# Memory rows in two groups, half copies, weights by chunk: one change to a fused attention and gated-FFN kernel

## The chip, the cores and the metric

The kernel runs on one core of one Trainium2 chip. The time is device microseconds of one execution; before the change three executions took 1120.69, 1125.61 and 1126.81 us, median 1125.61. A separate execution was profiled. Engines are named as in the profile: PE is the matrix engine (PEld its weight loads), DVE the vector engine, ACT the scalar engine, POOL the GpSimd engine, SP the sync engine, which issues most transfers. A "q" after an engine's name means the transfers that it issues.

## The reference

`x` is (2048, 640). A layer norm is followed by attention with a recurrent memory, a residual sum, a second layer norm, a gated FFN and a second residual sum:

```python
mem = mem0                                        # 8 rows
for s in range(64):                               # segments of 32 tokens
    h = concat([mem, xs])                         # 40 rows, 640 wide
    q, k, v = h @ Wq, h @ Wk, h @ Wv              # 32 heads of 128
    p = softmax(where(mask, q @ k.T * scale, -1e9))
    o = (p @ v) @ Wo
    mem = o[:, :8]                                # goes into the next segment
    outs.append(o[:, 8:])
h2 = h + (relu(xn @ W_gate) * (xn @ W_up)) @ W_down    # xn = layernorm(h), F = 1728
```

All weights and results are bf16. Only the 8 memory rows are serial: segment s+1 can't begin before the 8 rows of segment s have been through the output projection.

## The kernel before, in words

Everything is written by hand as a list of operations with keys of what they read and write. `_Graph.solve` turns the keys into semaphore waits, and each engine runs its operations in the order in which they were added. There is no scheduler: an operation that waits holds everything behind it on its engine. PSUM keys are whole banks (512 fp32 columns), and one bank's readers on different engines follow each other in program order.

**Start.** SP loads the first 64 and the next 128 rows of x, then the projection weights W (K, Q, V, each in two halves of 2560 KB) and the output weights Wo (two halves of 2560 KB), in this order on one queue. ACT issues the load of mem0. The first segments' tokens are normalised and projected while the weights come in.

**Passes.** One pass per segment, `s` = 0 to 63, in the loop over `NSEG`. A pass holds the 8 memory rows plus 24 token rows ("riders") of later segments, so that 32 columns of the array are filled; the tokens' last quarter is done by `extra_units` as filler. In PE's order a pass is: project K (`project`, 5 chunks of 128 rows x 2 halves x 4 matmuls of 512 columns), project Q, project V chunks 0 and 1, `pick_mem` (the memory rows' Q), V chunks 2 to 4, `scores`, two filler parts, `pv_mem` (first part with Vr, the older tokens' V; second with Vp, the memory rows' own), two filler parts, `trans_om` (transposes of the attention result of the memory rows into PSUM), a last filler part, `wo_pass` (the output projection, 128 small matmuls in two halves of 64), `pv_x` (attention of the segment's tokens). The next pass begins with K. In passes with `s % 4 == 1` the filler is `woe_pass`; in the others it is one of the three projections of the last quarter of tokens.

**What the other engines do in between.** After `scores`, ACT takes the exponentials of the memory part (`exp_mem`, into om), copies V bank P2 into Vp (`to_v`), and takes the exponentials of the token part (`exp_x`); DVE masks the first into Pbd in two instructions, one for each part of `pv_mem`. DVE copied V bank P3 into Vp before that. After `trans_om` DVE copies the transposes into oT in one instruction; `wo_pass` waits for it. After `wo_pass` `to_act` transposes the 160 columns of its result on DVE (`TBf`) and casts the 8 memory columns of each of the 5 chunks into `act_r`; the next pass's K waits for that. ACT stores the row form (`wtok`), DVE normalises `pv_x`'s result (`norm_x`: rx, then ox twice) and then copies half of K's result (`tok`) when K is done. K, Q and ox are turned around by transposing transfers on SP's queue (KS, QS, oT). POOL issues the copies of the riders' V rows (`v_riders`).

**PE's instruction stream.** `align` pads PE's stream with spare weight loads so that multiples of 256 instructions fall at chosen places (`MARKS`). In the DMA part of the profile the instruction queue carries 202 packets and 3.31 MB, which is one packet of 16 KB per 256 instructions of PE.

**Tail.** In pass 62 POOL loads the FFN's gate and up weights over the Q weights (`load_gate_up`: xn2T, Wg, Wgu, Wu, Wgu). After pass 63's attention PE runs the output projection of pass 62 (source QS, in two halves with a transpose between), that of pass 63 (source oT), the last `woe_pass`, and then four `gate_up` groups of block 0. SP loads the rows of block 1, and POOL h and the down weights, when Wu has landed.

**FFN.** Four blocks of 512 tokens. `gate_up` makes 14 chunks of 128 hidden units; the last holds 64 and takes partitions 64 to 127. `down` sums the 14 chunks for 128 tokens in two halves of 320 columns. In chunks 0 to 12 the second half is issued by `again`, which uses the weights already loaded; chunk 13 works on 64 partitions and loads its weights for each half.

Of the kernel before, what the change touches and what calls it, by code (L numbers as in the profile page):

```python
# [206 lines left out]
def build_kernel(nc, A_x, A_mem0, A_Wq, A_Wk, A_Wv, A_Wo, A_seg_len, B_W_gate, B_W_up, B_W_down, out):  # L207
# [134 lines left out]
    add("dve", lambda v: v.memset(oT[:], 0.0), w=[("oT", "m"), ("oT", "x")])  # L342
    add("pool", lambda p: p.memset(ap(Vp, Dh, [[VW, 8], [1, VW - Dh]]), 1.0), w=[("Vp1",)])
    for i in range(2):
        add("pool", lambda p, i=i: p.memset(act_r[i][:], 0.0),
            w=[("act", i, j, "m") for j in range(4)] + [("act", i, "x")])
# [82 lines left out]
    def to_v(b, t, i, key, eng):  # L429
        copy_op(eng, v_dst(t, i), bank(b).rearrange("p (k d) -> p k d", d=128), [B(b)], [key])  # L430

    def v_dst(t, i):
        return ap(t, 4 * i * VW, [[VW, 4], [1, 128]])
# [53 lines left out]
    def v_riders(t0, n):  # L487

        done = 0
        while done < n:  # L490
# [3 lines left out]
            for g in range(4):  # L494
                a, z = 32 * g + M + done, 32 * (g ^ 1) + o
                dma(Vr[q][z:z + m, :, :], Vp[a:a + m, :, :], r=[("Vp",), ("Vp1",), ("Vr1", q)],
                    w=[("Vr", q, g, o)], eng="pool")
# [8 lines left out]
    def ln1_load(b, buf, key):  # L506
        t0, n = (0, 64) if b < 0 else (64 + 128 * b, min(128, S - 64 - 128 * b))
        dma(buf[0:n, :], x_ap[t0:t0 + n, :], w=[key])
# [4 lines left out]
    def ln1_back(b, src, r, eng):  # L513
# [8 lines left out]
        if b < 0:  # L522
            for e in range(2):
                copy(act_r[1][:, e, :, :], src[:, :, 32 * e:32 * e + 32], [("act", 1, e, "m"), ("act", 1, "x")])
            return
# [11 lines left out]
    def pass_act(s):  # L537
        b, j = s // 4, s % 4
        return act_r[b % 2][:, j], [("act", b % 2, j, "m"), ("act", b % 2, "x", j), ("act", b % 2, "x")]
# [5 lines left out]
    def to_act(s, wkey, src):  # L545

        b, j = s // 4, s % 4
        add("dve", lambda v: v.transpose(TBf[:].rearrange("p c t -> p (c t)"), src), r=[wkey], w=[("TBf",)])  # L548
        add("dve", lambda v: v.tensor_copy(act_r[b % 2][:, j, :, 0:M], TBf[:, :, 0:M]), r=[("TBf",)],  # L549
            w=[("act", b % 2, j, "m")])  # L550
# [42 lines left out]
    def pv_mem(s):  # L593
        q = seg_slot(s)
        for a in range(2):
# [8 lines left out]
            add("pe", f, r=[("Pbd", a)] + ([("Vp",), ("Vp1",)] if a else vr_keys(q)), w=[B(T1)])  # L604
# [7 lines left out]
    def trans_om(tile):  # L612
        def f(pe):
            for a in range(2):
                for c in range(0, 128, tile):
                    i = pe.matmul(bank_bf(T1)[c:c + tile, a * 128:(a + 1) * 128], om[:, a, c:c + tile],  # L616
                                  ident[:, :], is_transpose=True)
            return i
        add("pe", f, r=[("om",), ("ident",)], w=[B(T1)])
        copy_op("dve", ap(oT, 0, [[2 * SEG, 8], [16 * SEG, 2], [SEG, 2], [1, M]]),  # L620
                bank_bf(T1)[:, 0:256].rearrange("p (k g e q) -> p k g e q", k=8, g=2, e=2), [B(T1)], [("oT", "m")])
# [8 lines left out]
    def wo_pass(bk, mark=None, src=oT, keys=(("oT", "m"), ("oT", "x")), halves=(0, 1)):  # L630
        for hf in halves:
# [7 lines left out]
            op = add("pe", f, r=list(keys) + [("Wo", hf)], w=[B(bk)])  # L639
# [24 lines left out]
    def pv_x(s, b0):  # L664
# [16 lines left out]
        add("pe", f, r=[("Px",), ("Pbd", 0), ("Pbd", 1), ("Vp",), ("Vp1",)] + vr_keys(q), w=[B(b0 + g) for g in range(4)])  # L681
# [11 lines left out]
    def trans_ox():  # L693
        dma_t(oT[:].rearrange("p h t -> p (h t)").rearrange("p (k r) -> p k r", r=128),
              ox[:].rearrange("p k g d -> p (k g d)"), [("ox", 0), ("ox", 1)], [("oT", "m"), ("oT", "x")])
# [14 lines left out]
    def copy_oTe(s):  # L710
        o = M * (s % 4)
        copy_op("dve", oTe[:, :, o:o + M], oT[:, :, 0:M], [("oT", "m")], [("oTe", s % 4)])
# [13 lines left out]
    def ln2_load(i):  # L726
        u = i % 4
        dma(xt2[u][:, :], x_ap[128 * i:128 * i + 128, :], r=[("Wdone", 1), ("Wu",)], w=[("xt2", u)])
        load_attn(at2[u], i, [("Wdone", 1), ("Wu",)], ("at2", u))
# [14 lines left out]
    ln1_load(-1, xt, ("xt",))  # L744
    ln1_load(0, x0, ("oTe", 0))
# [32 lines left out]
    a0, k0 = pass_act(0)  # L778
    groups = [(a0, k0)] + [(act_r[1][:, e], [("act", 1, e, "m"), ("act", 1, "x")]) for e in range(2)]
# [38 lines left out]
    for i in range(2):  # L818
        for n, (a, ks) in enumerate(groups):
            q = seg_slot(n - 1)  # L820
            t, key = (Vr[q], ("Vr", q)) if n else (Vp, ("Vp",))
# [364 lines left out]
```

## Time and profile before

| | us |
|---|---|
| median of three executions | 1125.61 |
| profiled execution, its own time | 1116.98 |
| its span | 1115.3 |
| start, up to 64 us: PE busy | 33.80 of 64.00 |
| passes 1 to 61 and the beginning of 62, 64 to 904 us: PE busy | 829.46 of 840.00 |
| change-over, 904 to 931 us: PE busy | 20.36 of 27.00 |
| FFN, 931 to 1116 us: PE busy | 180.32 of 185.00 |

PE's busy time overlaps itself, since matmuls are pipelined: a row "0.39 PE ... x4" is four matmuls of 512 columns in four column groups at once, and the next four start 0.22 us later. So waits of PE are read from the distance between starts and not from the busy share. In the timeline a row has its start, its length, engine, line, operation, what it writes and reads, the tile, and, in brackets, the idle time of that engine before it with what ended it. Line 397 is the reuse of loaded weights in `again`, and lines 461 (DVE) and 459 (ACT) are the copies in `copy_op`, so these are told apart by their tiles.

### The profile page before, as it was taken

To read this page: it belongs to the slowest core of one execution; us is meant where nothing else is said; L and a number is where in the kernel's file an instruction comes from. 1 tells how busy PE (TensorE), PEld (TensorE's weight loads), DVE (VectorE), ACT (ScalarE), POOL (GpSimd) and SP (SyncE) were. 2 spreads that over 40 slices of the span, in tenths; PEclk is the share of its full clock that TensorE was granted. 3 is DMA by queue.
4 is the path that set the end of the run, shared out by engine and by line. 5 is a ranking of instruction groups with operands and counts; after the bars stand their busy time and mean duration, and the time that the engine had idled before them with its cause. 6 is when DMAs were issued, how large, how long until landed. Compare 5 with 4: busy or idle time off the path is not lost.

```text
span 1115.3 us, 55631 instructions
## 1 busy us (share of the span) xinstructions
PE 1063.9 (95%) x28054; PEld 508.5 (46%) x23495; DVE 594.2 (53%) x1479; ACT 354.7 (32%) x732; POOL 286.3 (26%) x575
## 2 busy tenths in 40 slices
PE   4679999999999999999999999999999988999998
PEld 3344444444544454445454444444444455343443
DVE  3235555565556565666565656565656552463422
ACT  2213333334333333333333333333343422131220
POOL 1013333333333332323232323241424231000000
PEclk9979999999999999999999999999999999999999
DMA  9935464645454645465555565555545465122100
GB/s 352 380 85 106 91 109 85 105 90 107 85 108 82 109 80 111 80 124 102 117 106 112 107 111 111 98 102 96 100 92 92 88 198 178 42 77 77 24 18 24
DMA packets 287656, 121.61 MB, mean 109 GB/s; under 512 B 263840, under 2 KB 277056, under 8 KB 287424
## 3 DMA queue, kind: packets, MB, share of 16 engines
q1 hardware_dynamic: 268048, 94.16, 39.2%
q0 software_dynamic: 19184, 23.89, 9.4%
q8 instruction: 202, 3.31, 1.2%
q14 instruction: 30, 0.25, 0.1%
q10 hardware_dynamic: 192, 0.01, 0.0%
HBM read 36.79 MB, written 7.21 MB: 39 GB/s over the span
## 4 chain that ended last, share of the span: by engine, by line
PE 86%; DMA 6%; DVE 4%; SPq 3%; issue 1%; ACT 0%; DVEq 0%; ACTq 0%
PE ps L419 24%; PE ps L397 23%; PE ps L636 13%; PE ps L1021 10%; PE ps L1054 3%; PE ps L564 3%; PE ps L650 3%; SPq L357 3%; DMA QS<-tok 3%; DMA Wo<-in_A_Wo_dram 3%; PE ps L601 2%; DVE TBf L548 2%; PE ps L448 2%; PE ps L616 1%; DVE act_r L549 1%
## 5 line engine op out<-in xcount | busy, mean ns | idle before, releaser
L419 PE MATMUL ps<-W,act_r 128*32 128x512 bf16 x4277 | 395.0, 383 | 14.8 <-DMA W<-in_A_Wq_dram 3.0
L397 PE MATMUL ps<-W,act_r 128*32 128x512 bf16 x3603 | 352.6, 379 | 0.0
L357 POOL DMA_DIRECT2D Vr<-Vp x376 | 187.5, 506 | 466.9 <-ACT Vp L459 292.8
L419 PEld LDWEIGHTS ps<-W,act_r 128*32 128x32 bf16 x4277 | 115.4, 97 | 272.5 <-issue 213.3
L459 ACT ACTIVATE tok<-ps 128x512 bf16<-128x512 f32 x191 | 110.3, 594 | 257.0 <-PE ps L397 223.2
L461 DVE CAST tok<-ps 128x512 bf16<-128x512 f32 x131 | 90.6, 691 | 146.7 <-PE ps L397 121.5
L636 PE MATMUL ps<-Wo,oT 128*32 128x160 bf16 x8192 | 158.8, 236 | 10.3 <-DMA Wo<-in_A_Wo_dram 7.9
L636 PEld LDWEIGHTS ps<-Wo,oT 128*32 128x32 bf16 x8192 | 144.4, 98 | 36.0 <-DVE oT L461 24.9
L419 PE MATMUL ps<-W,act_e 128*32 128x512 bf16 x900 | 90.9, 381 | 0.0
L397 PE MATMUL ps<-W,act_e 128*32 128x512 bf16 x900 | 90.5, 379 | 0.0
L689 DVE TENSOR_TENSOR ox<-ps,rx 128x512 bf16<-128x512 f32 x128 | 82.5, 686 | 2.2
L459 ACT ACTIVATE Qr<-QS 128x512 bf16<-128x512 bf16 (+3 forms) x107 | 70.0, 682 | 31.7 <-DMA QS<-tok 31.2
L357 POOL DMA_DIRECT2D attn_d<-wtok x64 | 46.6, 729 | 115.0 <-ACT wtok L459 115.0
L548 DVE STREAM_TRANSPOSE TBf<-ps 128x160 f32<-128x160 f32 x64 | 22.4, 350 | 95.2 <-PE ps L636 95.1
L1021 PE MATMUL ps<-xn2T,Wg 128*128 128x512 bf16 x260 | 64.6, 379 | 0.0
L1021 PE MATMUL ps<-xn2T,Wu 128*128 128x512 bf16 x260 | 64.6, 379 | 0.0
L1036 DVE TENSOR_TENSOR hT<-g,ps 128x512 bf16<-128x512 bf16 (+1 forms) x56 | 38.5, 687 | 48.5 <-PE ps L1021 44.6
L574 ACT ACTIVATE om<-ps 128x128 bf16<-128x128 f32 x63 | 17.5, 277 | 146.0 <-PE ps L564 143.4
L1054 PE MATMUL ps<-Wd,hT 128*128 128x320 bf16 (+1 forms) x240 | 63.3, 300 | 0.0
L1034 ACT ACTIVATE g<-ps 128x512 bf16<-128x512 f32 (+1 forms) x56 | 32.4, 592 | 94.2 <-PE ps L1021 94.1
L461 DVE CAST Vp<-ps 128x512 bf16<-128x512 f32 x64 | 44.3, 692 | 31.0 <-PE ps L397 25.5
L397 PE MATMUL ps<-Wd,hT 128*128 128x320 bf16 x208 | 56.9, 299 | 0.0
(112 smaller groups left out, 1161.6 us busy)
## 6 DMA issues: line engine op xcount, KB each, us to landing
Vr<-Vp POOLq DMA_DIRECT2D x124, 48.8 KB, 1.9
W<-in_A_Wk_dram SPq DMA_DIRECT2D x2, 2560.0 KB, 13.4
W<-in_A_Wq_dram SPq DMA_DIRECT2D x2, 2560.0 KB, 25.6
W<-in_A_Wv_dram SPq DMA_DIRECT2D x2, 2560.0 KB, 27.3
Wo<-in_A_Wo_dram SPq DMA_DIRECT2D x2, 2560.0 KB
xt<-in_A_x_dram SPq DMA_DIRECT2D x30, 160.0 KB, 3.6
Vr<-Vp POOLq DMA_DIRECT2D x128, 32.5 KB, 1.9
attn_d<-wtok POOLq DMA_DIRECT2D x64, 40.0 KB, 2.8
```

Of the source, the lines that this page charges most:

```text
L357: add(eng, lambda e: e.dma_start(dst, src), r=r, w=w, dma=True)
L397: return pe.add_instruction(mybir.InstMatmult(name=nc.get_next_instruction_name(), engine=mybir.EngineType.PE, ins=[pe.lower_ap(rhs), pe.l ...
L419: ins = pe.matmul(*a, start=(c == 0), stop=(c == DC - 1), skip_group_check=True)
L459: add("act", lambda a: a.activation(dst, src, ACTF.Copy), r=r, w=w)
L461: add("dve", lambda v: v.tensor_copy(dst, src), r=r, w=w)
L548: add("dve", lambda v: v.transpose(TBf[:].rearrange("p c t -> p (c t)"), src), r=[wkey], w=[("TBf",)])
L564: i = pe.matmul(bank((P0, P1)[g % 2])[p:p + (M if a else 32), 40 * k:40 * k + 40], lh, Qr[:, h, q, :], start=True, stop=True, skip_group_c ...
L636: i = pe.matmul(bank(bk)[32 * gg:32 * gg + 32, 0:160], src[:, hb, :], w[:, gg], start=(hb == ORDER[0]), stop=(hb == ORDER[31]), skip_group ...
L689: add("dve", lambda v, kh=kh: v.tensor_tensor(ox[:, :, kh, :], src[:, :, kh, 0:128], ap(rx, kh, [[2, 4], [0, 128]]), ALU.mult), r=[B(b0 + ...
L1021: ins = pe.matmul(bank(bk), w[:, c, lo:lo + 128], xn2T[par][:, c, :], start=(c == 0), stop=(c == DC - 1))
L1036: add("dve", lambda v: v.tensor_tensor(hT[par][lo:128, j, :], g1[gi][lo:128, :], bank(bu)[lo:128, :], ALU.mult), r=[B(bu), ("g1", gi)], w= ...
L1054: i = pe.matmul(*a, start=(j == 0), stop=(j == FC - 1), skip_group_check=True)
```

## The change

Seven edits:

1. Keys of the memory rows in `act_r` are split: "m" for chunks 0 and 1, "n" for 2 to 4. `to_act` transposes and casts in two groups, and K's projection is two operations, the second of which waits for "n".
2. `trans_om` becomes two operations into two banks (T0 and P3, where T1 was), with two DVE copies of half the size into oT; the first half of `wo_pass` waits for the first copy and the second half for the second.
3. `to_v` of bank P2 on ACT is cut in two: half before `exp_mem`, half between `exp_mem` and `exp_x`. The keys of Vp are split, and ACT's part no longer follows DVE's.
4. The two first loads of x are issued by ACT, ahead of mem0, and not by SP.
5. Wg and Wu are loaded in five transfers each, one per chunk.
6. In the tail, `gate_up(0, 0)` goes ahead of pass 63's output projection and `gate_up(0, 1)` behind it; that projection uses bank P0 where it had bank 0.
7. The last down chunk covers all 128 partitions: DVE clears the lower 64 of hT (both buffers) and of Wd once, and the second half reuses the loaded weights as in the other chunks.

```diff
 def to_act(s, wkey, src):
-    add("dve", lambda v: v.transpose(TBf[:]..., src), r=[wkey], w=[("TBf",)])
-    add("dve", lambda v: v.tensor_copy(act_r[b % 2][:, j, :, 0:M], TBf[:, :, 0:M]), r=[("TBf",)], w=[("act", b % 2, j, "m")])
+    for n, (lo, hi) in enumerate(((0, 2), (2, DC))):
+        add("dve", lambda v, lo=lo, hi=hi: v.transpose(TBf[:, lo:hi, :]..., src[:, 32 * lo:32 * hi]), r=[wkey], w=[("TBf", n)])
+        add("dve", lambda v, lo=lo, hi=hi: v.tensor_copy(act_r[b % 2][:, j, lo:hi, 0:M], TBf[:, lo:hi, 0:M]),
+            r=[("TBf", n)], w=[("act", b % 2, j, "mn"[n])])
...
-    project(a, ks, 1, (0, 1), BQ, spare=40)
+    project(a, ks, 1, (0, 1), BQ, (0, 1), spare=16)
+    ks = ks + kn
+    project(a, ks, 1, (0, 1), BQ, (2, 3, 4), spare=24)
...
 def trans_om(tile):
-    (one operation into bank T1, both halves; one copy of 256 columns into oT)
+    for a, b in enumerate((T0, P3)):
+        def f(pe, a=a, b=b):
+            for c in range(0, 128, tile):
+                i = pe.matmul(bank_bf(b)[c:c + tile, 0:128], om[:, a, c:c + tile], ident[:, :], is_transpose=True)
+            return i
+        add("pe", f, r=[("om",), ("ident",)], w=[B(b)])
+    for a, b in enumerate((T0, P3)):
+        copy_op("dve", ap(oT, 8 * SEG * a, ...), bank_bf(b)[:, 0:128]..., [B(b)], [("oT", "mn"[a])])
...
-            op = add("pe", f, r=list(keys) + [("Wo", hf)], w=[B(bk)])
+            op = add("pe", f, r=list(keys[hf]) + [("Wo", hf)], w=[B(bk)])
...
-            to_v(P3, Vp, 1, ("Vp",), "dve")
+            to_v(P3, Vp, 1, ("Vp", 3), "dve")
+            to_v(P2, Vp, 0, ("Vp", 0), "act", 0, 2)
             scores(s)
             exp_mem()
-            to_v(P2, Vp, 0, ("Vp",), "act")
+            to_v(P2, Vp, 0, ("Vp", 1), "act", 2, 4)
             exp_x()
...
-    ln1_load(-1, xt, ("xt",))
-    ln1_load(0, x0, ("oTe", 0))
+    ln1_load(-1, xt, ("xt",), "act")
+    ln1_load(0, x0, ("oTe", 0), "act")
...
-            dma(t[:, :, :], src.rearrange("(c p) f -> p c f", p=128)[:, :, 0:FM], r=free, w=[(("Wg", "Wu")[n],)], eng="pool")
+            for c in range(DC):
+                dma(t[:, c, :], src[128 * c:128 * c + 128, 0:FM], r=free, w=[(("Wg", "Wu")[n], c)], eng="pool")
...
     copy_oTe(s)
+    gate_up(0, 0)
     (loads of block 1, h and Wd)
-    wo_pass(BQ[0])
-    rows(BQ[0], 1, s)
+    wo_pass(P0)
+    rows(P0, 1, s)
+    gate_up(0, 1)
     woe_pass(P3, range(16))
     woe_sum(P3)
     woe_store(NSEG // 4 - 1)
-    for j in range(4):
-        gate_up(0, j)
+    gate_up(0, 2)
+    gate_up(0, 3)
+    for par in range(2):
+        add("dve", lambda v, par=par: v.memset(hT[par][0:FR, FC - 1, :], 0.0), r=[("Wdone", 2)], w=[("hT", par, FC - 1)])
+    add("dve", lambda v: v.memset(Wd[0:FR, FC - 1, :], 0.0), r=[("Wdone", 1)], w=[("Wd", 2)])
...
 def down(b, u):
-                    p0 = 0 if j < FC - 1 else FR
                     for hf in range(2):
-                        a = (bank(bks[hf])[:, 0:320], hT[par][p0:128, j, u * 128:(u + 1) * 128], Wd[p0:128, j, hf * 320:(hf + 1) * 320])
-                        if hf and not p0:
+                        a = (bank(bks[hf])[:, 0:320], hT[par][:, j, u * 128:(u + 1) * 128], Wd[:, j, hf * 320:(hf + 1) * 320])
+                        if hf:
```

## The prediction

> **What bounds the kernel now.** I read the page first, then the list of waits, then the timeline of one pass, of the change-over and of one `down`.
>
> ```profile
> span 1115.3 us, 55631 instructions
> PE 86%; DMA 6%; DVE 4%; SPq 3%; issue 1%; ACT 0%; DVEq 0%; ACTq 0%
> ```
>
> The second line is the chain that ended last. PE sets the time; DVE's 4% are the places where PE stands still for the memory rows. POOL and ACT wait longest in the list of waits, but they wait for PE. So the question is what each edit takes out of PE's gaps. Pass 30 in the timeline:
>
> ```profile
> 468.36 0.28 ACT L574 ACTIVATE om<-ps 128x128 bf16<-128x128 f32 x1 [2.62 <-PE ps L564]
> 468.54 0.59 ACT L459 ACTIVATE Vp<-ps 128x512 bf16<-128x512 f32 x1
> 468.67 0.49 DVE L577 TENSOR_TENSOR Pbd<-om,mbd 128x256 bf16<-128x256 bf16 x2 [0.29 <-ACT om L574]
> 469.02 0.30 PE L601 MATMUL ps<-Vr,Pbd 128*32 128x129 bf16 x8
> 469.27 0.30 PE L601 MATMUL ps<-Vp,Pbd 128*32 128x129 bf16 x8
> ...
> 470.64 0.39 PE L397 MATMUL ps<-W,act_e 128*32 128x512 bf16 x4
> 470.65 0.29 DVE L461 COPY oT<-ps 128x256 bf16<-128x256 bf16 x1 [0.40 <-PE ps L616]
> 470.99 2.40 PE L636 MATMUL ps<-Wo,oT 128*32 128x160 bf16 x128
> ...
> 473.44 0.35 DVE L548 STREAM_TRANSPOSE TBf<-ps 128x160 f32<-128x160 f32 x1 [1.21 <-PE ps L636]
> 473.74 0.23 PE L674 MATMUL ps<-Vp,Pbd 64*64 64x129 bf16 x4
> 473.83 0.18 DVE L549 CAST act_r<-TBf 128x40 bf16<-128x40 f32 x1
> 474.07 0.40 PE L419 MATMUL ps<-W,act_r 128*32 128x512 bf16 x4
> ```
>
> Three gaps. Four 512-column matmuls take 0.215 from start to start, so `wo_pass` could begin at 470.86; it begins 0.13 later, 0.05 after the oT copy ends. `pv_x`'s groups are 0.06 apart, so K could begin at 473.80; it begins 0.27 later, after transpose and cast. The second part of `pv_mem` begins 0.25 after the first, where eight such matmuls take 0.12: 0.13 lost. I measured the same distances in all passes between 64 and 904 us: K's gap is 0.26 in every one (61 passes, 15.9 us); `wo_pass`'s is 0.13 in 30 passes (s % 4 of 2 and 3), 0.04 in 15 with `woe_pass`, 0.01 in the rest, 4.9 us in all; `pv_mem`'s 0.13 in nearly all, 8.2 us. A pass takes 13.49 to 13.62.
>
> **The change part by part.**
>
> *K in two groups.* DVE's time has a fixed part and one per column. Copies of fp32 from PSUM take 0.425 for 256 columns and 0.691 for 512 (groups by shape): 1.04 ns a column, 0.16 fixed. The transpose's 0.350 for 160 columns is then 0.167 for columns and 0.183 fixed; with 64 columns 0.250. The cast of 16 columns instead of 40 takes 0.155 instead of 0.183. K's first group is ready 0.10 + 0.03 = 0.13 earlier. [...] The fixed part lands behind it: DVE ends `to_act` 0.28 to 0.4 later by the rows[...]. The second group is ready near 474.45, and PE needs it four times 0.215 after 473.94, at 474.8: no wait. What is queued behind on DVE is rx and ox, then the `tok` copy of K, before which DVE stood idle 0.90 (2.38 after K's start): 0.37 stay. Then comes the KS transfer with 0.15 to spare before `scores`; so cover for 0.5, at 62 times the excess beyond. Gain 62 x 0.125 = 7.7 us; bounds: 0.06 a pass (3.7, if the fixed part dominates more) and the whole gap (16).
>
> *oT by halves.* The first operation of `trans_om` is done 0.06 earlier (half of eight or two matmuls), and 128 columns from PSUM instead of 256 save 0.07 of the copy's 0.29 (0.425 for 512, 0.292 for 256 bf16 columns: 0.5 ns a column). 0.13 earlier is just the gap: 30 x 0.13 + 15 x 0.04 = 4.5, less a little, 4.4 us; between 2 and 4.9. The second copy ends about 0.2 later and is needed 1.16 later. DVE's extra 0.15 ends in its 1.21 idle before TBf.
>
> *V on ACT.* P2 is ready with P3, 0.56 to 0.72 before om in every pass, and ACT idles from 1.1 before om at least. 160 columns take 0.303 and 512 0.594, so a half takes 0.38, done before om. The new waits on ACT, ahead of the exponentials that PE needs, are for PE's V and for the older copies out of Vp, issued by 473.4 with 1.9 us to landing, eight us early. The other half ends at about 468.92 instead of 469.13. But is Vp what the second part of `pv_mem` waits for? Pbd's second instruction ends at 469.16, after Vp's copy, and DVE to PE takes 0.06 to 0.08 (the first ends at 468.96, PE starts at 469.02). So Pbd holds it without Vp too: gain 0 to 0.03 a pass; I take 0.01, 0.6 us. If it was ACT after all, up to 8 us.
>
> *Last down chunk.* One boundary:
>
> ```profile
> 963.05 0.30 PE L397 MATMUL ps<-Wd,hT 128*128 128x320 bf16 x1
> 963.27 0.11 PEld L1054 LDWEIGHTS ps<-Wd,hT 64*128 64x128 bf16 x2 [0.40 <-issue]
> 963.28 0.69 PE L1054 MATMUL ps<-Wd,hT 64*128 64x320 bf16 x3
> 963.80 0.30 PE L397 MATMUL ps<-Wd,hT 128*128 128x320 bf16 x1
> ```
>
> Between the two L397 rows lie four steps, 0.75; ordinary steps are 0.136 (962.77 to 963.05 is two): 0.54. So 0.21 goes, 16 times: 3.3 us, between 2.5 and 3.6. The three clears stand on DVE behind four `gate_up` groups, at 0.5 or less each (a 512-column clear takes 0.485), beside 1.5 us of idle per group: nothing.
>
> *Change-over.*
>
> ```profile
> 924.08 0.57 PE L636 MATMUL ps<-Wo,QS 128*32 128x160 bf16 x21 [1.64 <-issue]
> 924.43 2.04 PE L636 MATMUL ps<-Wo,oT 128*32 128x160 bf16 x107
> 927.82 0.58 PE L636 MATMUL ps<-Wo,oT 128*32 128x160 bf16 x21 [1.35 <-issue]
> ```
>
> 21 + 107 matmuls with a weight load each are 256 instructions, one packet of the instruction queue. So I read these stops as PE waiting for instructions while transfers fill the DMA engines: 3.74 us from one stop's end to the next. With `gate_up(0, 0)`, ten matmuls of 0.216, within those 256, PE needs 2.4 + 2.16 less a tenth, about 4.3 us, and the second stop (1.35) goes. The first stays. Weights: SP sees Wu landed at 923.13; PE reaches the group at about 924.5 and Wu at 925.5. Eight more POOL issues at about 0.5 (0.506 for Vr) put the last Wu issue from 909.2 to about 913; the 5 MB flow until about 922 at 340 to 400 GB/s either way. Behind POOL's issues only a store waits. Gain 1.4; bounds -1 (Wu late) and 3 (both stops).
>
> *Start.*
>
> ```profile
> 0.81 0.61 SPq L357 DMA_DIRECT2D xt<-in_A_x_dram  x1
> 2.10 1.16 SPq L357 DMA_DIRECT2D W<-in_A_Wk_dram  x2
> 60.71 2.33 PE L636 MATMUL ps<-Wo,oT 128*32 128x160 bf16 x64 [5.69 <-DMA Wo<-in_A_Wo_dram]
> ```
>
> The first 60 us are the weights' transfer at about 400 GB/s, and PE waits 5.69 for the last of it. W can be issued at 0.81 instead of 2.10; the 0.24 MB of x then share its time (0.6). Gain 0.7, between 0 and 1.3. [...] Even 3 us later the first projections end before Q's second half lands, for which PE idles 2.95: no loss.
>
> Sum: 7.7 + 4.4 + 0.6 + 3.3 + 1.4 + 0.7 = 18.1. The places of 256 in PE's stream come out the same within the passes (each wait and spare load counted in the built program), so no fetch moves there. The span goes from 1115.3 to 1097, the profiled execution from 1116.98 to about 1099. The median of the runs lies 8.6 above that execution; carried over, 1125.61 - 18.1 = 1107.5.
>
> **The rivals.**
>
> *More: the gaps close wholly.* If the transpose's fixed part is less than I think, or Vp was the wait, K's gap gives up to 16 and `pv_mem`'s up to 8: sum about 28, 1097. For: 0.13 is lost before Vp in every pass. Against: Pbd ends 0.03 after Vp.
>
> *Less: small pieces cost more.* At 0.06 a pass for K, 2 for oT, and nothing at the change-over and the start: 3.7 + 2 + 3.3 = 9, 1116.6. For: only one shape of the transpose is in the trace.
>
> *Not slower is wrong: DVE becomes late.* If the four small instructions of `to_act` take longer, K's `tok` copy, the KS transfer, Kr and so `scores` slip. The cover is 0.5 us against my 0.4. It must first eat 18.1 and 5.6 more, 0.38 a pass beyond the cover: an addition of 0.9 us; at 1.0 the time is 1138. For: DVE is busy 0.58 of a pass. Against: none of its rows of such size is above 0.25.
>
> *The last chunk and start alone work,* if PE's gaps are its own pace after a wait and not DVE's: 4 us, 1121.5. Against: both copies end 0.05 before PE starts.
>
> **How the numbers follow.** Likeliest 0.60 (its own range 1103 to 1113); more 0.17; less 0.15; only chunk and start 0.04; DVE late 0.04. Range 1098 to 1117. A measurement of this kernel tells about 0.5% (5.6 us) from no change: faster 0.92 (the first three), same 0.05, slower 0.03.
>
> **What would show it.** In the profile after: the transpose in two forms, near 0.25 and 0.28; K's start 0.13 to 0.15 after `pv_x`'s last group and not 0.27; `wo_pass` 0.22 after the filler; `pv_mem`'s two parts still 0.22 to 0.25 apart; DVE idle before K's `tok` copy near 0.4; pass periods near 13.2 to 13.4; `down` every 3.80 us instead of 4.02; one stop in the change-over. Wrong if `scores` begins to wait for KS, if a stop in `wo_pass` appears in each pass, or if PE waits for Wu in the first `gate_up`.

## The result and the profile after

The changed kernel takes 1111.08 us (median of four executions, 1108.31 to 1111.65) where the kernel before took 1123.91 on the same chip (four executions, 1120.69 to 1126.81): a ratio of 0.9882, 95% interval 0.9847 to 0.9917, so 12.8 us less. On a second chip, with more executions, it was 1110.88 against 1119.71: 0.992 (0.9907 to 0.9933), 8.8 us less. Both lie short of the 18.1 of the sum. 1111.08 lies 3.6 above the forecast of 1107.5 and inside the range.

The profiled execution of the changed kernel took 1111.65 us. Its page, first the span and then the chain that ended last:

```profile
span 1109.9 us, 56106 instructions
...
PE 86%; DMA 8%; SPq 3%; issue 1%; POOL 1%; DVE 1%; ACT 1%; DVEq 0%; ACTq 0%
```

DVE's share of the chain fell from 4% to 1%: PE no longer stands still for DVE's copies as it did. Pass 30 in the timeline (PE, DVE and ACT; columns: start, length, engine, line, operation, tiles, count, idle time before):

```profile
465.95 0.38 ACT L461 ACTIVATE Vp<-ps 128x256 bf16<-128x256 f32 x1
466.08 0.49 DVE L582 TENSOR_TENSOR Pbd<-om,mbd 128x256 bf16<-128x256 bf16 x2 [0.28 <-ACT om L579]
466.43 0.30 PE L606 MATMUL ps<-Vr,Pbd 128*32 128x129 bf16 x8
466.63 0.30 PE L606 MATMUL ps<-Vp,Pbd 128*32 128x129 bf16 x8
...
467.96 0.35 DVE L463 COPY oT<-ps 128x128 bf16<-128x128 bf16 x2 [0.35 <-PE ps L621]
468.00 0.39 PE L397 MATMUL ps<-W,act_e 128*32 128x512 bf16 x4
468.24 2.40 PE L641 MATMUL ps<-Wo,oT 128*32 128x160 bf16 x128
...
470.69 0.25 DVE L552 STREAM_TRANSPOSE TBf<-ps 128x64 f32<-128x64 f32 x1 [1.08 <-PE ps L641]
470.97 0.17 DVE L554 CAST act_r<-TBf 128x16 bf16<-128x16 f32 x1
470.99 0.23 PE L679 MATMUL ps<-Vp,Pbd 64*64 64x129 bf16 x4
471.06 0.28 DVE L552 STREAM_TRANSPOSE TBf<-ps 128x96 f32<-128x96 f32 x1
471.20 0.40 PE L419 MATMUL ps<-W,act_r 128*32 128x512 bf16 x4
471.36 0.17 DVE L554 CAST act_r<-TBf 128x24 bf16<-128x24 f32 x1
471.36 0.30 ACT L461 ACTIVATE wtok<-ps 128x160 bf16<-128x160 f32 x1 [1.85 <-DVE TBf L552]
```

K begins 0.21 after `pv_x`'s last group (470.99 to 471.20) where it was 0.33; `wo_pass` begins 0.24 after the filler (468.00 to 468.24) where it was 0.35; the second part of `pv_mem` begins 0.20 after the first where it was 0.25. The transpose is there in the two forms, 0.25 and 0.28. So the three edits inside a pass do what they were to do. The FFN's `down`, at a chunk boundary:

```profile
963.65 0.30 PE L397 MATMUL ps<-Wd,hT 128*128 128x320 bf16 x1
963.79 0.30 PE L1062 MATMUL ps<-Wd,hT 128*128 128x320 bf16 x1
963.93 0.30 PE L397 MATMUL ps<-Wd,hT 128*128 128x320 bf16 x1
964.06 0.30 PE L1062 MATMUL ps<-Wd,hT 128*128 128x320 bf16 x1
```

One step of 0.13 or 0.14 after another, without the weight loads of the half chunk. One `down` follows the other in 3.80 instead of 4.01.

**Where the time went.** To add up the whole span I cut it at the starts of `scores`, which is in every pass, and at the groups of the tail, in two profiles of each kernel (the second pair is from the experiments). A kernel has a usual period that its passes keep to when little disturbs them; it differs with `s % 4`, since the filler does: 13.54, 13.61, 13.48 and 13.49 us before (for `s % 4` of 0 to 3), 13.37, 13.43, 13.21 and 13.25 after. What passes took beyond the sum of these periods I call stops. Single passes are up to 0.18 shorter than these periods, so the stops are a net figure, and the split between them and the undisturbed time is good to some 2 us; the sum of the two rows is not touched by it.

| us | before, two profiles | after, two profiles | difference of the means |
|---|---|---|---|
| start, to `scores` of pass 2 | 86.52, 86.89 | 85.56, 85.24 | -1.3 |
| the 59 passes from there to `scores` of pass 61, undisturbed | 798.2 | 785.5 | -12.7 |
| stops in these 59 passes | 3.7, 7.4 | 18.0, 14.6 | +10.8 |
| `scores` of pass 61 to that of 63 | 24.91, 25.78 | 24.60, 26.59 | +0.3 |
| from there to the fifth `gate_up` group | 25.85, 25.58 | 24.10, 24.22 | -1.55 |
| to the first `down` | 20.50, 20.50 | 19.86, 20.50 | -0.3 |
| first `down` to the end | 155.61, 155.60 | 152.37, 152.36 | -3.24 |
| span | 1115.3, 1120.0 | 1109.9, 1109.0 | -8.1 |

The undisturbed passes gave 12.7 us. That this is to the digit the sum of 7.7, 4.4 and 0.6 that I had for them is luck, since the three parts measured differ from it (see below). But 10.8 came back as stops. The list of waits shows where they are: rows in which `wo_pass` waits for nothing that the profile shows ("issue"; columns: us in total, times, longest), after and then before:

```profile
PEld ps L641 <- issue: 19.2, 24, 6.0
PE ps L641 <- issue: 8.1, 15, 2.4
```

```profile
PEld ps L636 <- issue: 4.8, 8, 1.8
PE ps L636 <- issue: 3.2, 3, 1.6
```

Line 641 after is line 636 before. The count tells here, 24 against 8 on the weight loads and 15 against 3 on the matmuls; the two rows overlap, and both hold the tail's stops too, so the size is taken from the table. Of the 18.0 us of the first profile 11.6 fall on the 14 passes with `s % 4 == 1`.

**The change-over and the start.** The change-over on PE:

```profile
919.25 0.94 PE L641 MATMUL ps<-Wo,QS 128*32 128x160 bf16 x43
922.55 0.58 PE L641 MATMUL ps<-Wo,QS 128*32 128x160 bf16 x21 [2.37 <-issue]
923.29 1.03 PE L1030 MATMUL ps<-xn2T,Wg 128*128 128x512 bf16 x4 [0.16 <-DMA Wu<-in_B_W_up_dram]
...
925.33 1.84 PE L641 MATMUL ps<-Wo,oT 128*32 128x160 bf16 x94
927.43 0.80 PE L641 MATMUL ps<-Wo,oT 128*32 128x160 bf16 x34 [0.27 <-issue]
```

`gate_up(0, 0)` took the place of the second stop, which fell from 1.35 to 0.27; the first grew from 1.64 to 2.37; and PE waited 0.16 for Wu. At the start:

```profile
0.81 1.03 SPq L357 DMA_DIRECT2D W<-in_A_Wk_dram  x2
...
59.93 2.33 PE L641 MATMUL ps<-Wo,oT 128*32 128x160 bf16 x64 [5.73 <-DMA Wo<-in_A_Wo_dram]
```

W is issued at 0.81 and the last Wo half reaches PE at 59.93 instead of 60.71, 0.8 earlier.

### The profile page after: what moved, and what is told of

Same layout as the page of the kernel before. It is cut to its first block, busy times and chain, and to the rows that moved or that the text cites. A ratio compares the mean times of both kernels' runs of the same rounds, so it can differ in the third digit from the quotient of the medians.

```text
span 1109.9 us, 56106 instructions
## 1 busy us (share of the span) xinstructions
PE 1054.9 (95%) x28040; PEld 510.8 (46%) x23478; DVE 608.7 (55%) x1673; ACT 365.7 (33%) x794; POOL 290.5 (26%) x583
## 4 chain that ended last, share of the span: by engine, by line
PE 86%; DMA 8%; SPq 3%; issue 1%; POOL 1%; DVE 1%; ACT 1%; DVEq 0%; ACTq 0%
PE ps L419 24%; PE ps L397 23%; PE ps L641 13%; PE ps L1030 10%; PE ps L655 3%; PE ps L679 3%; PE ps L569 3%; PE ps L1062 3%; DMA Wo<-in_A_Wo_dram 3%; SPq L357 3%; PE ps L606 2%; DMA QS<-tok 2%; DMA KS<-tok 2%; PE ps L450 2%; PE ps L621 1%
## 5 line engine op out<-in xcount | busy, mean ns | idle before, releaser
L419 PE MATMUL ps<-W,act_r 128*32 128x512 bf16 x4277 | 399.1, 384 | 8.8 <-DMA W<-in_A_Wv_dram 2.5
L397 PE MATMUL ps<-W,act_r 128*32 128x512 bf16 x3603 | 356.9, 379 | 0.3
L419 PEld LDWEIGHTS ps<-W,act_r 128*32 128x32 bf16 x4277 | 121.5, 97 | 262.2 <-issue 170.2
L641 PE MATMUL ps<-Wo,oT 128*32 128x160 bf16 x8192 | 161.8, 236 | 14.6 <-DMA Wo<-in_A_Wo_dram 8.0
L641 PEld LDWEIGHTS ps<-Wo,oT 128*32 128x32 bf16 x8192 | 147.0, 98 | 36.6 <-issue 16.7
L419 PE MATMUL ps<-W,act_e 128*32 128x512 bf16 x900 | 89.6, 381 | 0.0
L397 PE MATMUL ps<-W,act_e 128*32 128x512 bf16 x900 | 89.1, 379 | 0.0
L552 DVE STREAM_TRANSPOSE TBf<-ps 128x64 f32<-128x64 f32 (+1 forms) x128 | 33.5, 262 | 93.9 <-PE ps L641 93.8
L461 ACT ACTIVATE Vp<-ps 128x256 bf16<-128x256 f32 (+1 forms) x126 | 48.5, 385 | 104.7 <-PE ps L397 102.2
L1030 PE MATMUL ps<-xn2T,Wg 128*128 128x512 bf16 x246 | 61.6, 379 | 1.1 <-issue 0.3
L397 PE MATMUL ps<-Wd,hT 128*128 128x320 bf16 x224 | 61.0, 299 | 0.0
L1062 PE MATMUL ps<-Wd,hT 128*128 128x320 bf16 x224 | 61.0, 299 | 0.0
```

Of the source, the lines that this page charges most:

```text
L397: return pe.add_instruction(mybir.InstMatmult(name=nc.get_next_instruction_name(), engine=mybir.EngineType.PE, ins=[pe.lower_ap(rhs), pe.l ...
L419: ins = pe.matmul(*a, start=(c == 0), stop=(c == DC - 1), skip_group_check=True)
L461: add("act", lambda a: a.activation(dst, src, ACTF.Copy), r=r, w=w)
L552: add("dve", lambda v, lo=lo, hi=hi: v.transpose(TBf[:, lo:hi, :].rearrange("p c t -> p (c t)"), src[:, 32 * lo:32 * hi]), r=[wkey], w=[(" ...
L641: i = pe.matmul(bank(bk)[32 * gg:32 * gg + 32, 0:160], src[:, hb, :], w[:, gg], start=(hb == ORDER[0]), stop=(hb == ORDER[31]), skip_group ...
L1030: ins = pe.matmul(bank(bk), w[:, c, lo:lo + 128], xn2T[par][:, c, :], start=(c == 0), stop=(c == DC - 1))
```

## The experiments

Each ratio is to the kernel before on the same chip, with its 95% interval.

### Which part brings what

One kernel with the three edits inside the passes (1 to 3) and the rest as before, one with the four at the ends (4 to 7), one the changed kernel once more, one the kernel before once more for a second profile, and one with edit 4 alone undone.

```diff
# edit 4 undone
-    ln1_load(-1, xt, ("xt",), "act")
-    ln1_load(0, x0, ("oTe", 0), "act")
+    ln1_load(-1, xt, ("xt",))
+    ln1_load(0, x0, ("oTe", 0))
```

Edits 1 to 3 alone:

> Edits 1 to 3 alone (K in two groups, oT by halves, V on ACT), start, tail and FFN as before. Theory A: 15 us come out of the gaps of the passes and about as much as 9 of it goes into stops, so 5 to 8 us are gained: 1115 to 1119 where the kernel before has 1124. If the parts add up as predicted (no stops): 12.7 us, 1111. If these edits gain nothing at all and the whole difference comes from start, tail and FFN: 1124.

Edits 4 to 7 alone:

> Edits 4 to 7 alone (x on ACT's queue, weights by chunk, gate_up among the projections, whole last down chunk), the passes as before. By the two traces: start 0.8, tail and FFN 6.0, so 6.8 us: 1117 where the kernel before has 1124. As predicted it would be 5.4 (3.3 + 1.4 + 0.7). PE's passes keep their old length, so no new stops by theory A.

The changed kernel again, the kernel before again, and edit 4 undone:

> The changed kernel as it is, beside the others on one chip, for its time and a second profile. If the first result (ratio 0.988) holds: 0.986 to 0.990 of the kernel before. From the runs of edits 1 to 3 alone (0.9939) and 4 to 7 alone (0.9998) the sum would be 0.9937.

> The kernel before as it is, for a second profile: its first profiled execution (1116.98) lies below nearly all of its timed runs. Theory: at a typical time (1121) its passes hold some 4 us more of stops at the places of 256 than in the first profile, at the same places as the changed kernel's, so the changed kernel's stops are more of the same and not of a new kind.

> The changed kernel with edit 4 undone: the two first loads of x on SP's queue again. As predicted it costs 0.7 to 0.9 us against the changed kernel. In the profile of edits 4 to 7 alone the passes took 839.6 us where the kernel before had 830.9 with the same instructions on PE: if moving x to ACT's queue is what slowed them, this kernel is 3 to 5 us faster than the changed one; if that was scatter, 0 to 1 us slower.

| kernel | us, median | ratio | stops in 59 passes, us |
|---|---|---|---|
| edits 1 to 3 | 1114.42 | 0.9939 (0.9918 to 0.996) | 14.2 |
| edits 4 to 7 | 1120.21 | 0.9998 (0.9983 to 1.0012) | 11.6 |
| all, again | 1110.88 | 0.992 (0.9907 to 0.9933) | 14.6 |
| all but edit 4 | 1110.45 | 0.9912 (0.9887 to 0.9937) | 10.5 |
| before, again | 1121.69 (one execution) | | 7.4 |

The edits inside the passes bring 0.61%, 6.8 us, of the 12.7 in the sum. The stops are there with them alone. The edits at the ends bring nothing that is measured, though their own stretches are shorter: from the `scores` of pass 63 to the end that kernel takes 196.13 us, against 201.97 in the first profile of before. That profile lost 8 us in passes whose PE program I had not touched, to stops (11.6). So the ends' gain is real in their own stretches, and in this profile it is paid back in the passes. The two halves would multiply to 0.9937, the whole measured 0.992 and 0.9882. Edit 4 makes no difference in the time that these few executions could show.

### Is it the length of the stretches between two fetches?

The stops have no named releaser and lie at places 256 instructions apart, so I took them for waits of PE for its own instructions. A place, here and below, is a point at which PE's stream crosses a multiple of 256 instructions. The first theory was that the shorter passes leave too little time between two places of 256. `MARKS` moves the places in `wo_pass` within a pass: 24 instructions later, and 16 earlier.

```diff
-    MARKS = (150, 98, 114, 130)
+    MARKS = (174, 122, 138, 154)     # and, in the second kernel, (134, 82, 98, 114)
```

> The changed kernel with the multiples of 256 in PE's instruction stream 24 instructions later in every pass (MARKS of 174, 122, 138, 154); the work is the same. Theory A: the gain that is missing in the passes went into stops of PE at these places, because the stretch of 256 instructions before or after them has become shorter than the time in which the next packet of instructions comes (about 3.7 us). By the trace after, the shortest undisturbed stretches are 3.30, 3.62 and 3.91 us (those that begin in wo_pass and end in K, s % 4 of 1, 2, 3) and about 3.6 (the one that ends in wo_pass of s % 4 of 1). Shifted by 24 they are 3.94, 4.26, 4.55 and about 3.4. So the stops in K behind s % 4 of 1 go, those in wo_pass of s % 4 of 3 and 0 too, and those in wo_pass of s % 4 of 1 grow from 0.45 to about 0.65 us: 6 to 10 us faster than the changed kernel, 1101 to 1105. Theory B (the stops are collisions of transfers that the change has moved, or DVE's tok copy and KS coming late): the packets come at other times, but the waits stay where they are: 1109 to 1113. Theory C (mere scatter between executions): 1109 to 1113, with stops at other places.

> The changed kernel with the multiples of 256 in PE's instruction stream 16 instructions earlier (MARKS of 134, 82, 98, 114). Theory A: the stretches from wo_pass to K become 2.87, 3.19 and 3.47 us (s % 4 of 1, 2, 3), 0.8, 0.5 and 0.2 under 3.7: with 15 of each some 22 us of stops, about 15 more than in the changed kernel, mostly in K: 1122 to 1132. Theories B and C: 1109 to 1113.

Measured: 1121.48, ratio 1.0008 (0.9993 to 1.0022), and 1118.66, ratio 0.998 (0.9967 to 0.9993), each over 22 executions. Both lose most of the gain; their profiled executions, which took 1126.8 and 1126.1 us of span, have 31.4 and 30.5 us of stops (they lie 7 and 9 us above the median of their kernel). So where the places lie is worth up to 10 us. In one stretch the theory holds: from the place in `wo_pass` to that in the next K, behind passes with `s % 4 == 1`. Undisturbed it takes 3.27 us in the changed kernel (3.38 before), 3.93 with the later places and 2.77 with the earlier ones, and K's stops there go and grow with it: 1.3 to 3.0 us in the changed kernel, 0.0 and 7.5 in these two. A stop in K with the earlier places (pass 29; the next row is due 0.22 after the first, and comes 0.54 after it):

```profile
463.50 0.39 PE L397 MATMUL ps<-W,act_r 128*32 128x512 bf16 x4
464.04 0.40 PE L419 MATMUL ps<-W,act_r 128*32 128x512 bf16 x4 [0.16 <-issue]
```

But with the later places, where these stops are gone, the time is no better: more is lost between `scores` and the end of `wo_pass`. So the length of the stretches is a cause, and not the only one.

The other is in the trace's records of single DMA packets. PE's instructions come in 202 packets of 16 KB; the 28040 matmuls and 23478 weight loads on the page of the changed kernel are about 201 times 256. A packet starts 1.0 to 1.2 us after PE has passed a place of 256 if nothing is in its way, takes 1.05 us (0.88 to 1.6), and where PE waits for it, PE goes on some 1.4 us after its end (1.2 to 1.6). That is about 3.5 us for a fetch. In passes with `s % 4 == 1` the stretch from the place in the filler to the place in `wo_pass` is 3.69 us undisturbed (3.78 before), so a fetch that starts 1.0 after the place is in time (1.0 + 1.05 + 1.4 = 3.45), and one that starts 1.7 after it is late by 0.46. The median start there:

| kernel | QS issued ahead of `scores`, us | packet starts after the place, us | stops in passes with `s % 4 == 1`, us |
|---|---|---|---|
| before, two profiles | 1.07, 1.05 | 1.00, 1.02 | 1.2, 3.9 |
| edits 4 to 7 | 0.86 | 1.24 | 4.0 |
| edits 1 to 3 | 0.89 | 1.34 | 6.3 |
| all but edit 4 | 0.77 | 1.39 | 6.6 |
| all, two profiles | 0.72, 0.55 | 1.73, 1.67 | 11.6, 8.6 |

What seems to lie in its way is QS, the transposing transfer of the riders' Q: by and large, the later it is issued, the later the packet starts. Pass 29, which is one of these, in the timeline: SP's transposing issues and `wo_pass` on PE, before:

```profile
450.07 1.24 SPq L360 DMA_TRANSPOSE KS<-tok  x1
451.36 1.33 SPq L360 DMA_TRANSPOSE oT<-ox  x1
452.77 1.26 SPq L360 DMA_TRANSPOSE QS<-tok  x1
457.51 2.40 PE L636 MATMUL ps<-Wo,oT 128*32 128x160 bf16 x128
```

and after:

```profile
446.74 2.02 SPq L360 DMA_TRANSPOSE KS<-tok  x1
448.81 1.30 SPq L360 DMA_TRANSPOSE oT<-ox  x1
450.20 1.27 SPq L360 DMA_TRANSPOSE QS<-tok  x1
454.10 1.07 PE L641 MATMUL ps<-Wo,oT 128*32 128x160 bf16 x52
455.84 1.50 PE L641 MATMUL ps<-Wo,oT 128*32 128x160 bf16 x76 [0.67 <-issue]
```

Before, PE passed the place in the filler at 454.51, 1.74 after the issue of QS, and its packet ran from 455.42 to 456.39. After, PE passed it at 451.18, only 0.98 after the issue of QS; the packets of QS ran from 451.4 to 453.4, the instruction packet started at 452.95, when the last of them were under way, and ended at 454.42, and PE stood from 454.94 to 455.84, in the middle of `wo_pass`. The records do not name the DMA engine of a packet, so that the one waited for the other is not seen directly.

The first row shows why QS comes later: the issue of KS took 2.02 instead of 1.24, and oT and QS are queued behind it on SP. Over all passes, in the groups by line (columns after the count: least, median and longest ns; first and last start), before and after:

```profile
L360 SPq DMA_TRANSPOSE KS<-tok x62: 1232/1238/2215, 67.5 to 898.2; - x62
```

```profile
L360 SPq DMA_TRANSPOSE KS<-tok x62: 1232/1403/2537, 67.0 to 898.7; - x62
```

The least is the same, the median is 0.17 longer. In the packet records a long issue meets an instruction packet: of the transposing issues over 1.5 us, 31 of 31 and 36 of 36 overlap one before (two profiles), 49 of 50 and 55 of 56 after, out of some 234 each. With a packet that starts within 0.1 us of the issue the mean is 1.6, at 0.3 to 0.5 into it 2.0, and beyond 0.8 it is 1.23 again. So I read it as the two holding each other: an instruction packet makes the issue of KS longer, QS comes later, and holds the next instruction packet. The first link rests on this coincidence in time alone. It does not explain the kernel with the places 24 later: the issue of KS took 1.7 on average in its passes with `s % 4 == 1`, and 1.6 and 1.8 in the two profiles of the changed kernel.

### QS taken out of the way

If QS is what holds the packet, the stops must go without it, or when it is issued elsewhere. First the riders' QS transfer left out from pass 3 on, which tells the mechanism apart and nothing else:

```diff
-            if nr and s < NSEG - 2:
+            if nr and s < 3:
                 trans_q()
```

> The changed kernel without the transposing transfer QS of the riders' Q from pass 3 on: the copy behind it takes what an earlier pass left there, so the riders' attention is not computed; PE's work and all other transfers are the same. Theory A': as the run with QS later or a little better, stops 4 to 8 us, 0.983 to 0.987. If the stops come from the shorter stretches, or from KS and oT alone: 0.990 to 0.993.

Measured: 1095.7, ratio 0.9791 (0.9767 to 0.9816), with 3.0 us of stops in the 59 passes: 4.7 in those with `s % 4 == 1`, and in sum less than none in the others, since without QS passes with `s % 4 == 0` take 13.23, 0.14 under the period counted as undisturbed. The packet in the filler of `s % 4 == 1` starts at 1.01. The waits of `wo_pass`, of which the tail's are a good part now:

```profile
PEld ps L641 <- issue: 12.3, 10, 6.9
PE ps L641 <- issue: 3.3, 4, 1.7
```

24 times became 10, and 15 became 4. To move QS within a complete kernel took three trials. The first put it behind the exponentials of the memory part, by an added read of om; the second mended that by a key that only the exponential writes.

```diff
-            if nr and s < NSEG - 2:
-                trans_q()
...
             exp_mem()
+            if nr and s < NSEG - 2:
+                trans_q([("om",)])       # second trial: trans_q([("exp",)])
```

> The changed kernel with one transfer later: the transposing transfer of the riders' Q (QS) is issued when the exponentials of the memory part are done (1.2 us behind the start of scores) and not 1.1 us ahead of scores. Theory A', from the packets in the traces: PE's next 256 instructions come in one 16 KB packet, which normally starts about 1.1 us after PE has passed a place of 256 and lets PE go on 1.45 us after its end, 3.6 us in all; where KS, oT and QS fill the DMA engines at that moment, the packet starts 0.5 to 0.9 later, and PE stands in wo_pass (of s % 4 of 1 above all). With QS out of the way the packet asked for at the beginning of scores starts near 1.1 again: stops in wo_pass fall from about 10 us to under 4, and the time by 5 to 9 us: 0.981 to 0.985 of the kernel before. Rival: if the stops come from the shorter stretches alone (3.3 to 3.6 us against a fixed time of the packet), nothing changes: 0.987 to 0.990. Rival: QS late holds ACT's copies behind it and through them the next K: slower than the changed kernel, with waits of PE for ACT.

> As the run before with QS later, but with the dependence mended: there QS read om itself, so norm_om, which overwrites om, had to wait for the transfer (4 us a pass). Here QS waits for a mark of its own that the exponentials set. Theory A' (PE's instruction packet waits behind the transposing transfers): the packet asked for at the beginning of scores starts 1.1 us later in all passes and not 1.5 to 2; the stops in the 59 passes, 14.6 to 18 us in the two profiles of the changed kernel, fall to 5 to 9, most of it in s % 4 of 1: 1102 to 1106, 0.984 to 0.988 of the kernel before. If the stops come from the shorter stretches alone: 0.991 to 0.993, as the changed kernel.

Measured: about 1424, ratio 1.2719 (1.2672 to 1.2765), and 1237.93, ratio 1.1072 (1.1031 to 1.1113); the granted clock in their profiles is 0.90 and 0.97, where it is 0.99 in the others, so the waits need not be the whole loss. In the first the transfer reads om, so DVE's normalisation of om had to wait until the transfer had landed, and `trans_om` waited for that. The list of waits:

```profile
ACT Qr L461 <- DMA QS<-tok: 245.6, 61, 4.7
DVE om L614 <- DMA QS<-tok: 229.3, 61, 4.4
PE ps L621 <- DVE om L614: 220.9, 63, 4.2
```

In the second no such wait is left, but QS runs beside the copies of the riders' V and lands 5.0 us after its issue (median; 3.2 in the changed kernel), and on ACT the copy Qr stands ahead of the `tok` copies. ACT in one pass:

```profile
416.99 0.84 ACT L461 ACTIVATE Qr<-QS 128x768 bf16<-128x768 bf16 x1 [4.55 <-DMA QS<-tok]
417.74 0.58 ACT L461 ACTIVATE tok<-ps 128x512 bf16<-128x512 f32 x1
```

So these two tell of what was queued behind the moved step, and not of the packets. The third trial issues QS behind `wo_pass`, in passes with `s % 4` of 0 and 1 only, and moves ACT's copy of it behind the next pass's `tok` copies; once in the changed kernel, once in the kernel before.

```diff
-            if nr and s < NSEG - 2:
+            if nr and s < NSEG - 2 and s % 4 > 1:
                 trans_q()
...
-                if s < NSEG - 2:
+                if s < NSEG - 2 and s % 4 > 1:
                     (copy of QS into Qr)
...
-            op = add("pe", f, r=list(keys[hf]) + [("Wo", hf)], w=[B(bk)])
+            nq[0] += 1
+            op = add("pe", f, r=list(keys[hf]) + [("Wo", hf)], w=[B(bk), ("wod", nq[0])])
...
         wo_pass(T1, ...)
+        if 0 < s < NSEG - 2 and s % 4 < 2 and nr:
+            trans_q([("wod", nq[0])])
+            late.append(lambda t0=t0, nr=nr: evac_q(QS, ("QS",), t0, nr, M, "act"))
```

> The changed kernel, complete, with the QS transfer of the passes with s % 4 of 0 and 1 issued behind wo_pass (5.9 us behind the start of scores, with nothing of ACT's behind it) and its copy into Qr in the next pass behind K's tok copies. In the profiles of the changed kernel these two classes hold 9.6 to 13.3 of the 14.6 to 18 us of stops. Theory A': without QS the packet asked for at the beginning of scores starts 1.0 us later and not 1.5 to 1.7, as in the run without QS, so most of these stops go: 4 to 9 us faster than the changed kernel, 0.984 to 0.988 of the kernel before. If QS itself, landing before KS is issued, disturbs KS or the packet of the next K: 0.990 to 0.994, no gain. If stops come from the shorter stretches: no gain either.

> The kernel before with the same move of QS alone. Its profiles hold 1.6 and 5.3 us of stops in the two classes. If the change is what brought packet and transfer together, there is little to win here: 0 to 4 us, 0.997 to 1.000. If the collision was there all along and the changed kernel only has the same stops: as much as there, 5 to 9 us, 0.992 to 0.995.

Measured: in the changed kernel 1105.55 (1103.37 to 1106.89), ratio 0.9858 (0.9836 to 0.988); in the kernel before 1118.32, ratio 0.9969 (0.9956 to 0.9982). The packet in the filler of `s % 4 == 1` starts at 1.04 in both, and the stops of the 59 passes fall to 6.8 and 0.8. Pass 29 of the changed kernel with QS behind `wo_pass`:

```profile
445.12 1.77 SPq L360 DMA_TRANSPOSE KS<-tok  x1
446.94 1.30 SPq L360 DMA_TRANSPOSE oT<-ox  x1
452.36 2.39 PE L641 MATMUL ps<-Wo,oT 128*32 128x160 bf16 x128
454.84 1.24 SPq L360 DMA_TRANSPOSE QS<-tok  x1
```

KS is still long (1.77), but PE passes the place in the filler at 449.44, the packet runs from 450.44 to 451.50, and `wo_pass` has no stop. This is the fastest complete kernel of the study: 15.5 us below the kernel before on its chip, where the changed kernel was 8.8 and 12.8 below on two others (the two were not run on one chip, and the first result's interval, 0.9847 to 0.9917, overlaps this one's). So the move is worth 2.7 to 6.7 us to the changed kernel and 2.8 to the kernel before. The theory needs that the changed kernel gains more, since it is there that QS had come into the way: the stops say so, 9.5 us against 4.7, but the times do not show it clear of the noise. And since the kernel before gains too, part of the collision was there already. In its profile the gain of 9.5 us of stops is not all kept: about 1.1 goes at the start, 1.6 between the `scores` of passes 61 and 63, and 2.0 behind them, so the span is 1104.6, 4.9 below the mean of the two of the changed kernel.

The two causes can be told apart by place. The table takes the time from the first to the last matmul of `wo_pass`, and from the first to the 37th of K, beyond the shortest of its kind in each profile:

| kernel | in `wo_pass`, 59 passes, us | in K behind `s % 4 == 1`, 14 passes, us |
|---|---|---|
| before, two profiles | 1.6, 5.3 | 0.3, 0.9 |
| all, two profiles | 10.6, 8.7 | 3.0, 1.3 |
| places 24 later | 14.9 | 0.0 |
| places 16 earlier | 8.9 | 7.5 |
| QS left out | 2.5 | 1.7 |
| QS behind `wo_pass` | 5.1 | 1.2 |
| before, QS behind `wo_pass` | 1.8 | 0.6 |

The stops in `wo_pass` go with QS (where it is issued behind `wo_pass` in half of the passes, the other half holds 3.4 of the 5.1). Those in K stay without it and follow the length of the stretch: at 3.27 us it is shorter than the 3.45 of a fetch that nothing holds.

## Why the prediction was right and wrong

- *K in two groups, 7.7.* Right. K begins 0.11 us nearer to `pv_x`'s last group (0.32 to 0.21), 6.5 us over the 59 passes that I added up, where 0.125 was taken. The transpose of 64 columns took 0.249 on average, as the fixed part of 0.183 gave. DVE idles 0.61 before K's `tok` copy in an undisturbed pass, where I had some 0.4, and KS was not late through DVE: the rival "DVE becomes late" is out.
- *oT by halves, 4.4.* Right: 4.3 by the distances. `wo_pass` begins 0.57 after the transposes instead of 0.69 in 30 passes, and 0.04 and 0.01 earlier in the others.
- *V on ACT, 0.6.* The size was wrong: 3.0, from 0.25 to 0.20 between the two parts of `pv_mem` in nearly every pass. I had read that Pbd, ending 0.03 after Vp, holds the second part. In the profile after, PE starts 0.06 after Pbd ends (466.57 to 466.63), before it was 0.11, so I take it that Vp had held it by 0.05: with 0.03 between two ends, the rows did not tell which the reader waited for.
- *The rival "more"* adds up wrongly: with K at 16 and `pv_mem` at 8 the sum is 33.8, and not about 28. Nothing hangs on it, since neither came near.
- These three make 13.8, and the undisturbed passes are 12.7 shorter. The 1.1 between (0.02 a pass) I did not find.
- *Last down chunk, 3.3.* Right: 3.24 from the first `down` to the end.
- *Change-over, 1.4.* Right in its sum, 1.55, but not in its course: the first stop, which "stays", grew by 0.7, and the second shrank by 1.1 and did not go. The sign "PE waits for Wu" came true, at 0.16.
- *Start, 0.7.* Right: 0.8 at the last half of Wo. x came later, as I had allowed for: with W's transfer under way its two first loads landed 6.1 and 7.3 after their issue instead of 2.3 and 2.7, it is normalised from 6.94 instead of 4.42 and the first K comes at 15.18 instead of 12.30, and neither is on the path that sets the end.
- *The step that failed:* "The places of 256 in PE's stream come out the same within the passes, so no fetch moves there." The places came out the same in the stream. But what matters is when PE passes them, beside the transposing transfers of the pass: the transposing transfers and the fetches came to lie on each other, one stretch between two places fell from 3.38 to 3.27 us, and the stops went from a mean of 5.5 to 16.3 us. I had looked at the fetches only in the change-over, where the timeline showed them. The records do not name the DMA engine of a packet, so why an instruction packet starts late beside QS is not shown. The stops came to 3.7 to 18.0 us in the 59 passes, in two profiles of each kernel.
- *The sign "wrong if a stop in `wo_pass` appears in each pass"* came true in about a quarter of the passes, mostly those with `s % 4 == 1`.
- *The carry-over.* I set the sum against a median of 1125.61 from three executions. Later medians of the kernel before were 1119.71 to 1121.08 on four chips. The forecast of the time came out only 3.6 us low although the gain was 5 to 9 us smaller, because of that: the closeness is luck.

What stays open. Why KS and the fetches of instructions meet more often after the change was argued and not tried: ACT's store copy `wtok` now waits for DVE's second transpose (both read one bank), begins 0.16 after K's start where it began 0.24 before, and POOL issues the store of it at 0.76 instead of 0.36 after K's start (medians of 59 passes, the same in two profiles each); the packets asked for in K behind `s % 4` of 1 to 3 start 0.2 to 0.5 later after their place than before. That wait is new, and I had not listed it. Second, the kernel with the edits at the ends only has PE's old program in the passes and still 11.6 us of stops in its profile; two profiles of the kernel before differ by 3.7 themselves, so this may be chance or not. Third, why stops between `scores` and the end of `wo_pass` grow with the places 24 later is not known. Fourth, undoing edit 4 gave fewer stops in one profile (10.5 against 14.6 and 18.0) and no time that differs.

## What to carry to other kernels

Count the instruction packets as transfers of the kernel: this PE stream had 202 of them, one per 256 instructions, and the shorter passes moved them against the other transfers (in pass 29 the place in the filler came 0.98 us after QS's issue, before it was 1.74). So read when PE passes each place, how long it takes to the next, and what DMA is under way until the packet has come (1.9 and 3.2 us after the place in pass 29, before and after). Before crediting a gain inside a repeated pass, look for rows that wait for "issue" in it, and leave room for them to grow. A transfer with slack, such as QS here, can be placed behind the critical stretch and not ahead of it, if what is queued behind it and behind its copy is moved as well; done halfway it made the kernel 118 and some 305 us slower than before.

## What the runs showed of the hardware

- A fetch of PE's instructions took about 3.5 us from the place to PE's going on: 1.0 to 1.2 until the packet of 16 KB starts, 1.05 for the packet, some 1.4 after its end. Where PE came to the next place of 256 sooner than that, it stopped: stretches of 3.93, 3.27 and 2.77 us that end in K gave 0.0, 1.3 to 3.0, and 7.5 us of stops in 14 passes.
- With QS, a transposing transfer, issued 0.55 to 0.72 us ahead of `scores` the packet started 1.7 us after the place (medians), with QS left out or moved 1.0.
- Issues of a transposing transfer on SP that met an instruction packet 0.3 to 0.5 us after their start took 2.0 us on average, single ones up to 2.5, where those without one took 1.23 to 1.33, and what is queued behind them on SP came that much later.
- DVE's transpose of fp32 from PSUM took 0.35, 0.28 and 0.25 us for 160, 96 and 64 columns: by these figures some 0.18 of it is fixed. Its cast of 16, 24 and 40 columns took 0.18 each: nearly all of it is fixed.
